# One operand of each routing step on VectorE in a bank of PSUM, in a kernel of attention, dense layers and routed experts

## The chip, the cores and the metric

The kernel runs on one core of one Trainium2 chip. The metric is the device time of one execution in microseconds (us). The engines are called PE (TensorE), DVE (VectorE), ACT (ScalarE), POOL (GpSimd) and SP (SyncE).

## What is computed

The reference chains three parts. First, attention over 4 batches and 8 heads with 1152 keys of 64 elements, where pairs of queries are averaged to 576. Then a dense block on the 2304 resulting tokens of 512 elements: `h = (x w1) * (x w2)`, `x2 = h w3 w_out`. Last, a mixture of 8 experts. The routing is greedy over all 2304 x 8 logits and is what the change touches:

```python
logits = x @ w_gate
order = np.argsort(-logits.flatten())
for idx in order:
    tok, e = (int(idx) // E, int(idx) % E)
    if assigned[tok] >= 0 or counts[e] >= cap:
        continue
    assigned[tok] = e
    counts[e] += 1
```

Each expert gets `cap` = 288 tokens and computes `relu(x w1[e]) w2[e]` for them.

## The kernel before, in words

**Who orders the work.** Nothing is issued in the order of the text. Every operation is handed to `Sched.op` (line 184) with its engine or engines, a cost in ns, a priority, and the keys that it reads and writes. `Sched.run` (line 214) then plays a model of the four engines with these costs and the latencies of `Sched.LAT`, always starts the ready operation of the lowest priority number, and emits the instructions of each engine in the order found. On the chip each engine's queue runs in that fixed order. Costs of `c_dve` (line 320) don't depend on what POOL does. The helper `call` of line 113 issues most instructions from attention onwards, so the trace shows L113 for them and groups are told apart by tile names.

**PSUM.** There are eight banks. Four, `pts` (tiles `pt0` to `pt3`, made at the start of `attention_moe_experts_kernel`), are handed out through `Slots` and `Hold`: an operation that `takes` a hold gets a free bank in the model, and the bank is free again after the hold's last user. The other four are `pb`, for matrix products. After attention the `pt` banks serve transposes (gathered rows into an expert, and an expert's result back into rows), the counts and small sums of the routing, the slot lists, and the products of the hidden units 4 up to `AHEAD` - 1 of expert 0 (line 1626). `AHEAD` is 7 (line 1723). With it, the products of units 0 to 6 with the left half of the gathered rows (`firsts`, line 1638) come before those with the right half.

**Stages from about 770 us on.** (1) The product W = w3 w_out on PE, split into two parts by ACT (`Wh`) and POOL (`Wl`). (2) x2 = h W, in 18 tiles of 128 tokens, with h split by ACT (`x2h`) and POOL (`x2l`). (3) The 8 experts: `unit` (line 1525) loads 128 rows of a weight into `u` and splits them into `uh` (ACT or DVE) and `ul` (DVE or POOL, u minus uh); `gather` (line 1584) fetches the expert's tokens by an indirect DMA on POOL's queue, transposes them on PE and splits them into `exh` and `exl`; `expert` (line 1621) multiplies on PE, splits the hidden units into `ehh` (ACT) and `ehl` (DVE), multiplies again, transposes back and scatters by an indirect DMA.

**Routing** (`routing`, line 853) runs beside all of these, with priority 1900 (W has 2000, x2 2010, the experts 3000). It has 8 phases. In a phase each token points to its best expert that is not full (`rt_m`, `rt_mu`, `rt_t`, `rt_mx`, `rt_oh`), and the logit value at which the first expert becomes full is found by a search in 8 rounds of 4 bits: 15 thresholds at a time are made (`rt_thr`, `rt_G`), all tokens are compared with them (`rt_mask`), PE counts by a matmul of `rt_oh` and `rt_mask`, DVE takes the right blocks out (`rt_cnt`, `rt_sum`, `rt_own` for the tile `rt_own8`), PE sums over partitions, and DVE finds how many thresholds hold (`rt_any`, `rt_flag`, `rt_n`) and extends the prefix (`rt_base`). After the rounds the phase assigns tokens and closes the expert (`rt_ge`, `rt_rows`, `rt_inc`, `rt_y`, `rt_r`, `rt_pen`, `rt_al`, `rt_acc`, `rt_s`, `rt_U`, `rt_rem`, `rt_pend`); `pick` chooses which closed expert is computed next and writes the row of its weights for SP's register; `lists` (in `slot_lists`, line 1069) turns the assignment into the indices `idx` of the gather. All of it is a chain of small fp32 or int32 instructions on DVE with two PE round trips per round, and all of its tiles lie in SBUF, but for what PE writes. The trace drops digits at the end of names: `rt_t` is t8 or t9, `rt_r` is r2, `rt_M` M or M1, `rt_acc` ac or ac2.

The tiles come from small rings; `make_ring` (line 130) hands out each name's buffers in turn, and the buffer is the key by which the planner orders readers and writers.

Of the kernel before, what the change touches and what calls it, by code (L numbers as in the profile page):

```python
# [11 lines left out]
F32 = mybir.dt.float32  # L12
# [839 lines left out]

def routing(nc, sch, rp, slots, c, L, keyL, A, rows_of, idx, prio, prio_l):

# [5 lines left out]
    def ring(name, n, shape, dt):  # L860
        return make_ring(sch, rp, "rt_" + name, n, shape, dt)

    r_m, r_mu = ring("m", 2, [128, NC], F32), ring("mu", 2, [128, NC], F32)
    r_t8, r_oh = ring("t8", 2, [128, NC, 8], F32), ring("oh", 2, [128, NC, 8], BF16)
    r_mx, r_mask = ring("mx", 1, [128, NC], F32), ring("mask", 2, [128, NC, NTHR], BF16)
    r_flag, r_any, r_n = ring("flag", 2, [128, NTHR], F32), ring("any", 2, [128, NTHR], F32), ring("n", 2, [128, 1], I32)
    r_cnt, r_sum = ring("cnt", 2, [NCG * NTHR, NCG, 8], F16), ring("sum", 2, [NCG * NTHR, 8], F16)
    own8 = rp.tile([97, NTHR, 8], F16, name="rt_own8")
    r_base, r_thr, r_G = ring("base", 2, [128, 1], I32), ring("thr", 2, [128, NTHR], I32), ring("G", 2, [128, NTHR], I32)
    r_M, r_M1 = ring("M", 1, [128, 1], I32), ring("M1", 1, [128, 1], I32)  # L870
    r_ge, r_rows = ring("ge", 1, [128, 2, 8, NC], F32), ring("rows", 1, [128, 16], BF16)
    r_inc, r_y = ring("inc", 1, [128, 8, NC], F32), ring("y", 1, [128, 8, NC], F32)
    r_r2, r_pen = ring("r2", 1, [128, 8], F32), ring("pen", 1, [128, 8], F32)
    r_al, r_acc, r_s = ring("al", 1, [128, 8], F32), ring("acc", 2, [128, 8, NC], F32), ring("s", 1, [128, NC], F32)
    U, keyU = ring("U", 1, [128, NC], F32)()
    rem, keyR = ring("rem", 1, [128, 8], F32)()
    pend, keyP = ring("pend", 1, [128, 8], F32)()
    r_sc, r_top, r_own = ring("sc", 1, [128, 8], F32), ring("top", 1, [128, 1], F32), ring("own", 2, [128, 8], F32)

    def dve(n, fn, r, w, engine="DVE", uses=(), pr=prio):  # L880
        sch.op(engine, c_dve(n) if engine == "DVE" else c_pool(n), fn, r=r, w=w, prio=pr, uses=uses)
# [4 lines left out]
    dve(120, lambda: nc.vector.memset(own8, 0.0), [], ["own8", "own8r"])  # L886
    dve(144, lambda: nc.vector.memset(A, 0.0), [], ["A"])
    dve(144, lambda: nc.vector.tensor_scalar(L, L, -1e34, 1e34, op0=OP.max, op1=OP.min), [keyL], [keyL])

    def pick(n):  # L890

        (sc, ksc), (top, kt), (own, ko) = r_sc(), r_top(), r_own()
        dve(8, lambda: nc.vector.scalar_tensor_tensor(sc, pend, 0.5, c["wd"], op0=OP.is_gt, op1=OP.mult), [keyP], [ksc], pr=P_PICK)
        dve(8, lambda: nc.vector.tensor_reduce(top, sc, axis=AX.X, op=OP.max), [ksc], [kt], pr=P_PICK)
        dve(8, lambda: nc.vector.tensor_scalar(own, sc, top, None, op0=OP.is_equal), [ksc, kt], [ko], pr=P_PICK)
        dve(8, lambda: nc.vector.tensor_tensor(pend, pend, own, op=OP.subtract), [keyP, ko], [keyP], pr=P_PICK)
        dve(4, lambda: nc.vector.scalar_tensor_tensor(
            rows_of[n], top[:, :].to_broadcast([128, 4]), -512.0, c["row"], op0=OP.mult, op1=OP.add), [kt], [("rows_of", n)], pr=P_PICK)
        return own, ko

    lists = slot_lists(nc, sch, rp, slots, c, A, idx, prio, prio_l)
    for ph in range(8):
# [6 lines left out]
        dve(18, lambda m=m, mu=mu: nc.vector.tensor_tensor(mu, m, U, op=OP.add), [km, keyU], [kmu])  # L909
        t8, kt8 = r_t8()  # L910
        dve(144, lambda m=m, t8=t8: nc.vector.tensor_tensor(
# [9 lines left out]
        if ph < 7:  # L921
# [4 lines left out]
            for rd, b in enumerate(BITS):  # L926
                T = 2 ** b - 1
                mask, kma = r_mask()
                if rd == 0:
                    thr, kth = c["t0"], "t0"  # L930
                else:
                    thr, kth = r_thr()
                    if rd == 1:
                        dve(T, lambda thr=thr, T=T, rd=rd, base=base: nc.vector.tensor_scalar(
                            thr[:, :T], c["grid"][rd][0], base, None, op0=OP.bitwise_xor), [kb], [kth])
                    else:
                        dve(T, lambda thr=thr, n=n, sh=sh, G=G: nc.vector.scalar_tensor_tensor(
                            thr, n[:, :].to_broadcast([128, NTHR]), sh, G, op0=OP.logical_shift_left, op1=OP.bitwise_xor), [kn, kG], [kth])
                    if rd + 1 < len(BITS):
                        G, kG = r_G()  # L940
                        dve(T, lambda G=G, rd=rd, base=base: nc.vector.tensor_scalar(
                            G, c["grid"][rd + 1][0], base, None, op0=OP.bitwise_xor), [kb], [kG])
# [63 lines left out]
            def f(ps=ps, rows=rows):  # L1006
# [3 lines left out]
            sch.op("PE", 40, f, r=[kro], takes=ps, prio=prio)  # L1010
            inc, kin = r_inc()
            dve(288, lambda ge=ge, inc=inc: nc.vector.tensor_tensor_scan(
# [17 lines left out]
                rem, pen, -1e-27, r2, op0=OP.mult, op1=OP.add), [kpe, kr2], [keyR])  # L1030
            ac, kac = r_acc()
            dve(144, lambda y=y, al=al, ac=ac: nc.vector.tensor_tensor(
# [12 lines left out]
        else:  # L1045
            un, kun = r_s()
            dve(18, lambda un=un: nc.vector.tensor_scalar(un, U, 0.0, None, op0=OP.is_equal), [keyU], [kun])
            t8, kt8 = r_t8()
            dve(144, lambda oh=oh, un=un, t8=t8: nc.vector.tensor_tensor(
# [18 lines left out]

def slot_lists(nc, sch, rp, slots, c, A, idx, prio, prio_l):

# [4 lines left out]

    r_all, r_s, r_rows = ring("all", 1, [128, NC, 8], F32), ring("s", 2, [128, NC], F32), ring("rows", 2, [128, 1], BF16)
    r_inc, r_pre, r_slot = ring("inc", 2, [128, NC], F32), ring("pre", 2, [128, 1], F32), ring("slot", 2, [128, NC], F32)
    r_ge, r_g, r_r = ring("ge", 2, [128, NC, 4], F32), ring("g", 2, [128, NC], F32), ring("r", 2, [128, NC], F32)
    r_oh, r_og = ring("oh", 1, [128, NC, 96], BF16), ring("og", 1, [128, NC, 3], F32)
# [59 lines left out]
def moe_and_experts(tc, sch, env, w1, w2, w3, w_out, w_gate, e1, e2, out):  # L1139
# [276 lines left out]
    rows_of = [rreg.tile([128, 4], I32, name=f"rows{n}") for n in range(8)]  # L1416
    routing(nc, sch, rreg, s_pt, rc, L, "L", A, rows_of, idx, P_R, P_L)

# [303 lines left out]
LIST_SLACK, RT_SLACK = 0.0, 0.0  # L1722
AHEAD = 7
HELD = 4
# [6 lines left out]
def attention_moe_experts_kernel(ctx, tc, q, k, v, w1, w2, w3, w_out, w_gate, e1, e2, out):  # L1731
# [10 lines left out]
    for r in regions.values():  # L1742
# [9 lines left out]
    env = {"nc": nc, "G": G, "xT": xT, "main": regions["main"], "prep": regions["prep"], "psS": regions["psS"],  # L1752
           "s_pt": s_pt, "ident": ident, "rc": rc, "xreg": regions["x"], "x2": dpool.tile([N, DM], F32, name="x2"), "x2a": dpool.tile([N, DM // 2], F32, name="x2a"), "w3t": dpool.tile([8, 128, 2, 1024], F32, name="w3t"),
           "wof": dpool.tile([8, 128, 2, DM], F32, name="wof")}
# [28 lines left out]
```

## Time and profile before

| | |
|---|---|
| median of 3 runs | 1267.52 us (1264.34 to 1271.21) |
| the profiled execution, its own time | 1259.13 us |
| its span, first to last instruction | 1257.3 us |
| mean granted clock of PE over the span | 0.977 |
| instructions | 24260 |
| the chain that ended last, by engine | PE 72%, DVE 21% |

The profile is of one execution. A page sums busy time by engine and groups instructions by line, engine, operation and tiles (`out<-in`). "Idle before" is the time that the engine waited just before such instructions, and the name behind an arrow is what ended most of it. Durations are those of one instruction from start to end; neighbours on an engine overlap by some tens of ns. [...] The chain that ended last is followed back from the last instruction: at each step to what released it, or to the instruction before it on its engine.

### The profile page before, as it was taken

What the parts mean: (1) busy time and instruction counts of PE and PEld (TensorE: products, weight loads), DVE (VectorE), ACT (ScalarE), POOL (GpSimd) and SP (SyncE); (2) the same over time, 40 slices, a digit from 0 to 9 for tenths busy, and PEclk for the clock granted to TensorE, in tenths of its full rate; (3) what the DMA queues carried; (4) which work ended last, traced back from release to release, by engine and by line L of the source; (5) the groups of instructions that cost most, each with busy time, mean ns of one, the idle gap of its engine ahead of it and who ended that gap; (6) DMA issues with size and microseconds to landing.
All of it is one profiled execution on the core that took longest, in us unless ns stands there. A gap on an engine that the chain in (4) does not pass through costs nothing.

```text
span 1257.3 us, 24260 instructions
## 1 busy us (share of the span) xinstructions
PE 1168.0 (93%) x8377; PEld 1099.2 (87%) x8377; DVE 1042.1 (83%) x2966; ACT 629.3 (50%) x1322; POOL 638.9 (51%) x649
## 2 busy tenths in 40 slices
PE   6999999999999999899999999988898868888997
PEld 4999999999999999899999998766677868888996
DVE  7999999999999999988777876778777988988741
ACT  6888888888888888333222202132221533322321
POOL 4566666666666765444332343264435654453730
PEclk9999999999999999899999999999997989998999
DMA  9676666666666541144555523432224644451620
GB/s 211 148 172 144 156 157 155 153 154 155 155 156 160 119 101 54 62 166 169 185 168 168 185 68 124 154 95 55 57 64 131 219 153 135 143 172 51 226 81 26
DMA packets 116618, 169.88 MB, mean 135 GB/s; under 512 B 47959, under 2 KB 79710, under 8 KB 116494
## 3 DMA queue, kind: packets, MB, share of 16 engines
q1 hardware_dynamic: 113326, 158.89, 46.9%
q0 software_dynamic: 3168, 9.44, 2.3%
q8 instruction: 66, 1.08, 0.4%
q14 instruction: 58, 0.48, 0.1%
HBM read 104.87 MB, written 24.45 MB: 103 GB/s over the span
## 4 chain that ended last, share of the span: by engine, by line
PE 72%; DVE 21%; issue 2%; DMA 2%; POOL 1%; ACT 1%; SPq 0%; DVEq 0%; POOLq 0%; ACTq 0%
PE pb L113 32%; PE s L590 12%; PE pt L614 7%; PE pt L664 6%; PE pt L113 5%; PE s L664 5%; PE s L614 3%; DVE ul L113 2%; DVE cv_v L113 2%; DVE rt_base L113 1%; DVE rt_flag L113 1%; DVE uh L113 1%; DVE rt_own L113 1%; DVE p L600 1%; DVE rt_mask L113 1%
## 5 line engine op out<-in xcount | busy, mean ns | idle before, releaser
L600 DVE TENSOR_SCALAR_CACHE_REDUCE p<-s 128x384 f32<-128x384 f32 x432 | 229.9, 551 | 32.6 <-PE pt L614 12.1
L590 PE MATMUL s<-kst,qst 128*128 128x384 f32 x768 | 198.7, 357 | 7.5 <-DVE p L600 4.0
L605 ACT ACTIVATE p<-p,mn 128x1152 f32<-128x1152 f32 x144 | 181.2, 1258 | 25.3 <-DVE mn L603 23.2
L113 PE MATMUL pb<-xhi,wh 128*128 128x288 f32 x512 | 156.6, 306 | 1.7 <-ACT wh L113 1.7
L113 PE MATMUL pb<-xlo,wh 128*128 128x288 f32 x512 | 152.5, 298 | 2.0 <-DVE xlo L113 2.0
L113 PE MATMUL pb<-xhi,wl 128*128 128x288 f32 x512 | 152.2, 297 | 1.1 <-DVE wl L113 1.1
L590 PEld LDWEIGHTS s<-kst,qst 128*128 128x128 f32 x768 | 122.5, 189 | 14.0 <-DVE p L600 10.6
L614 PE MATMUL pt<-ident,p 128*128 128x128 f32 x879 | 132.1, 272 | 0.3 <-ACT p L605 0.3
L113 POOL TENSOR_TENSOR ul<-u,uh 128x512 fp32r<-128x512 f32 (+1 forms) x45 | 88.9, 1984 | 77.7 <-ACT uh L113 30.2
L648 DVE TENSOR_TENSOR p_lo<-pt,p_hi 128x384 fp32r<-128x384 f32 x230 | 124.6, 551 | 0.7 <-ACT p_hi L331 0.7
L331 ACT ACTIVATE p_hi<-pt 128x384 fp32r<-128x384 f32 x230 | 106.6, 492 | 12.3 <-PE pt L614 12.1
L614 PEld LDWEIGHTS pt<-ident,p 128*128 128x128 f32 x879 | 106.8, 140 | 4.4 <-ACT p L605 0.5
L113 DVE SCALAR_TENSOR_TENSOR cv_v<-cv_raw,cv_v 128x512 int32<-128x512 int32 (+1 forms) x120 | 102.1, 856 | 6.7 <-POOL cv_raw L113 4.6
L113 PEld LDWEIGHTS pb<-xlo,wh 128*128 128x128 f32 x512 | 97.3, 190 | 2.8 <-DVE xlo L113 2.8
L113 PEld LDWEIGHTS pb<-xhi,wh 128*128 128x128 f32 x512 | 97.4, 190 | 2.6 <-ACT wh L113 1.9
L113 PEld LDWEIGHTS pb<-xhi,wl 128*128 128x128 f32 x512 | 97.3, 190 | 1.3 <-DVE wl L113 1.3
L341 POOL TENSOR_TENSOR p_lo<-praw,p_hi 128x384 fp32r<-128x384 f32 x96 | 96.9, 1017 | 0.4
L113 ACT ACTIVATE a<-pb 128x288 f32<-128x288 f32 x64 | 26.2, 410 | 132.4 <-PE pb L113 123.6
L335 POOL CAST p_hi<-praw 128x384 fp32r<-128x384 f32 x96 | 47.5, 506 | 83.3 <-ACT praw L331 83.2
L113 POOL TENSOR_TENSOR cv_raw<-cv_raw 128x512 f32<-128x512 f32 x40 | 43.2, 1079 | 86.5 <-DVE cv_v L113 67.3
L113 PE MATMUL pb<-exh,uh 128*128 128x288 f32 x244 | 78.6, 322 | 6.3 <-DVE ehl L113 6.3
L113 PE MATMUL pb<-ehh,uh 128*128 128x288 f32 x256 | 80.6, 315 | 0.0
(316 smaller groups left out, 3386.3 us busy)
## 6 DMA issues: line engine op xcount, KB each, us to landing
u<-in_moe_w_dram SPq DMA_DIRECT2D x64, 512.0 KB
cv_raw<-in_moe_w_dram SPq DMA_DIRECT2D x32, 512.0 KB
vr<-in_v_dram SPq DMA_DIRECT2D x32, 288.0 KB
kr<-in_k_dram SPq DMA_DIRECT2D x32, 288.0 KB
kst<-kH SPq DMA_DIRECT2D x31, 288.0 KB
kst<-kL SPq DMA_DIRECT2D x31, 288.0 KB
qr<-in_q_dram SPq DMA_DIRECT2D x15, 576.0 KB
w3t<-wg SPq DMA_DIRECT2D x16, 512.0 KB
```

The source lines that it names most:

```text
L113: return f(*[x.get() if isinstance(x, Lazy) else x for x in a], **{n: x.get() if isinstance(x, Lazy) else x for n, x in k.items()})
L331: nc.scalar.activation(out, in_, AF.Copy)
L335: nc.gpsimd.tensor_copy(out, in_)
L341: (nc.vector if eng == "DVE" else nc.gpsimd).tensor_tensor(out, a, b, op=OP.subtract)
L590: nc.tensor.matmul(ps.tile[:, :384], a[:, :], b[:, cs], start=(n == 0), stop=(n == len(passes) - 1))
L600: sch.op("DVE", c_dve(384), lambda ps=ps, c=c, cs=cs: nc.vector.tensor_scalar(t[:, cs], ps.tile[:, :384], 1.0, BIG, op0=OP.mult, op1=OP.mi ...
L605: sch.op("ACT", c_act(S, psum=False, acc=True), lambda: nc.scalar.activation(t, t, AF.Exp, bias=mn[:, 3:4], scale=-1.0, accum_out=sm[0][:, ...
L614: nc.tensor.transpose(ps.tile[:, a * 128:(a + 1) * 128], t[:, b * 128:(b + 1) * 128], ident)
L648: sch.op("DVE", c_dve(384), lambda view=view, src=src: nc.vector.tensor_tensor(view(lo), src(), view(hi).bitcast(F32), op=OP.subtract), us ...
L664: nc.tensor.matmul(ps.tile[:, :n], vt[:, t, :, :], src[half][:, t, off:off + n], start=(half == 0 and t == 0), stop=(half == 1 and t == NT ...
```

## The change

Most small tiles of the routing and the lists move from SBUF into one bank of PSUM, `pts[3]`: a new helper `in_bank` cuts them from the bank's 512 words per partition, words 0 to 143 being shared by the three large ones (`rt_t8p`, `rt_incp`, `rt_acp`), which live one after the other. They are chosen so that of two operands of a step one lies in the bank. Where a step reads two large tiles, its first result goes to the bank and its second stays in SBUF (t8 to the bank, t9 to SBUF; ac and ac2 alike). `rt_sum` becomes fp32 (it was fp16), several rings go from two buffers to one, and two constants, the grid of round 1 and the weights `wd`, are copied into the bank at the start. From the routing on, `Slots` is made of the first three banks alone, and `AHEAD` goes from 7 to 6. The computation is the same.

```diff
+def in_bank(bank, name, n, shape, dt, at=None):
+
+    size = int(np.prod(shape[1:]))
+    if at is None:
+        at = bank[1]
+        bank[1] += n * size
+        assert bank[1] <= 512
+    state = [0]
+
+    def nxt():
+        i = state[0] % n
+        state[0] += 1
+        t = bank[0][:shape[0], at + i * size:at + i * size + size]
+        t = t if dt == F32 else t.bitcast(dt)
+        t = t if len(shape) == 2 else t.rearrange("p (a b) -> p a b", a=shape[1])
+        return t, (name, i)
+    return nxt
...
-def routing(nc, sch, rp, slots, c, L, keyL, A, rows_of, idx, prio, prio_l):
+def routing(nc, sch, rp, slots, bank, c, L, keyL, A, rows_of, idx, prio, prio_l):
...
-    r_m, r_mu = ring("m", 2, [128, NC], F32), ring("mu", 2, [128, NC], F32)
-    r_t8, r_oh = ring("t8", 2, [128, NC, 8], F32), ring("oh", 2, [128, NC, 8], BF16)
-    r_mx, r_mask = ring("mx", 1, [128, NC], F32), ring("mask", 2, [128, NC, NTHR], BF16)
-    r_flag, r_any, r_n = ring("flag", 2, [128, NTHR], F32), ring("any", 2, [128, NTHR], F32), ring("n", 2, [128, 1], I32)
-    r_cnt, r_sum = ring("cnt", 2, [NCG * NTHR, NCG, 8], F16), ring("sum", 2, [NCG * NTHR, 8], F16)
+    at = lambda name, n, shape, dt: in_bank(bank, "rt_" + name, n, shape, dt)
+    r_m, r_mu = at("m", 1, [128, NC], F32), at("mu", 1, [128, NC], F32)
+    r_t8p, r_acp, r_incp = (in_bank(bank, "rt_big", 1, [128, NC * 8], F32, 0) for _ in range(3))
+    r_t8, r_oh = ring("t8", 1, [128, NC, 8], F32), ring("oh", 2, [128, NC, 8], BF16)
+    r_mx, r_mask = at("mx", 1, [128, NC], F32), ring("mask", 2, [128, NC, NTHR], BF16)
+    r_flag, r_any, r_n = at("flag", 1, [128, NTHR], F32), at("any", 1, [128, NTHR], F32), ring("n", 2, [128, 1], I32)
+    r_cnt, r_sum = ring("cnt", 2, [NCG * NTHR, NCG, 8], F16), at("sum", 1, [NCG * NTHR, 8], F32)
...
-    r_base, r_thr, r_G = ring("base", 2, [128, 1], I32), ring("thr", 2, [128, NTHR], I32), ring("G", 2, [128, NTHR], I32)
-    r_M, r_M1 = ring("M", 1, [128, 1], I32), ring("M1", 1, [128, 1], I32)
+    r_base, r_thr, r_G = at("base", 2, [128, 1], I32), ring("thr", 2, [128, NTHR], I32), at("G", 2, [128, NTHR], I32)
+    r_M, r_M1 = at("M", 1, [128, 1], I32), ring("M1", 1, [128, 1], I32)
+    (grid1, _), (wd, _) = at("grid1", 1, [128, NTHR], I32)(), at("wd", 1, [128, 8], F32)()
...
-    r_inc, r_y = ring("inc", 1, [128, 8, NC], F32), ring("y", 1, [128, 8, NC], F32)
-    r_r2, r_pen = ring("r2", 1, [128, 8], F32), ring("pen", 1, [128, 8], F32)
-    r_al, r_acc, r_s = ring("al", 1, [128, 8], F32), ring("acc", 2, [128, 8, NC], F32), ring("s", 1, [128, NC], F32)
+    r_y = ring("y", 1, [128, 8, NC], F32)
+    r_r2, r_pen = ring("r2", 1, [128, 8], F32), at("pen", 1, [128, 8], F32)
+    r_al, r_acc, r_s = at("al", 1, [128, 8], F32), ring("acc", 1, [128, 8, NC], F32), at("s", 1, [128, NC], F32)
...
-    r_sc, r_top, r_own = ring("sc", 1, [128, 8], F32), ring("top", 1, [128, 1], F32), ring("own", 2, [128, 8], F32)
+    r_sc, r_top, r_own = at("sc", 1, [128, 8], F32), at("top", 1, [128, 1], F32), at("own", 2, [128, 8], F32)
...
+    dve(NTHR, lambda: nc.vector.tensor_copy(grid1, c["grid"][1][0]), [], ["rt_consts"])
+    dve(8, lambda: nc.vector.tensor_copy(wd, c["wd"]), [], ["rt_consts"])
...
-        t8, kt8 = r_t8()
+        t8, kt8 = r_t8p()
+        t8 = t8.rearrange("p (c e) -> p c e", e=8)
...
-            inc, kin = r_inc()
+            inc, kin = r_incp()
+            inc = inc.rearrange("p (e c) -> p e c", e=8)
...
-            ac, kac = r_acc()
+            ac, kac = r_acp()
+            ac = ac.rearrange("p (e c) -> p e c", e=8)
...
-def slot_lists(nc, sch, rp, slots, c, A, idx, prio, prio_l):
+def slot_lists(nc, sch, rp, slots, bank, c, A, idx, prio, prio_l):
...
-    r_all, r_s, r_rows = ring("all", 1, [128, NC, 8], F32), ring("s", 2, [128, NC], F32), ring("rows", 2, [128, 1], BF16)
-    r_inc, r_pre, r_slot = ring("inc", 2, [128, NC], F32), ring("pre", 2, [128, 1], F32), ring("slot", 2, [128, NC], F32)
-    r_ge, r_g, r_r = ring("ge", 2, [128, NC, 4], F32), ring("g", 2, [128, NC], F32), ring("r", 2, [128, NC], F32)
+    at = lambda name, n, shape, dt: in_bank(bank, "sl_" + name, n, shape, dt)
+    r_all, r_s, r_rows = ring("all", 1, [128, NC, 8], F32), at("s", 1, [128, NC], F32), ring("rows", 2, [128, 1], BF16)
+    r_inc, r_pre, r_slot = ring("inc", 2, [128, NC], F32), ring("pre", 2, [128, 1], F32), at("slot", 2, [128, NC], F32)
+    r_ge, r_g, r_r = ring("ge", 2, [128, NC, 4], F32), ring("g", 2, [128, NC], F32), at("r", 1, [128, NC], F32)
...
-    routing(nc, sch, rreg, s_pt, rc, L, "L", A, rows_of, idx, P_R, P_L)
+    bank = [env["pts"][3], 144]
+    s_pt = Slots(env["pts"][:3])
+    routing(nc, sch, rreg, s_pt, bank, rc, L, "L", A, rows_of, idx, P_R, P_L)
...
-AHEAD = 7
+AHEAD = 6
```

## Rows read from the trace of the kernel before

**Rows 1.** The page, part 1: busy us and share of the span by engine.

```profile
PE 1168.0 (93%) x8377; PEld 1099.2 (87%) x8377; DVE 1042.1 (83%) x2966; ACT 629.3 (50%) x1322; POOL 638.9 (51%) x649
```

**Rows 2.** Windows: stretch, length, busy us by engine, granted clock, DMA share.

```profile
770.00:830.00 60.00, 54.13 (x273) 40.95 (x271) 44.94 (x160) 16.29 (x28) 22.82 (x21) 0.98 0.48 156
830.00:945.00 115.00, 103.76 (x568) 80.11 (x568) 86.66 (x307) 29.57 (x52) 52.23 (x44) 0.98 0.24 56
945.00:1150.00 205.00, 165.74 (x1235) 158.77 (x1234) 180.40 (x496) 65.17 (x125) 106.32 (x87) 0.91 0.45 146
1150.00:1257.00 107.00, 96.36 (x750) 94.80 (x749) 55.07 (x113) 27.75 (x54) 41.31 (x44) 0.96 0.34 113
```

**Rows 3.** PE's waits, 770 us on: us in total, times, longest.

```profile
PE pt L113 <- DVE rt_mask L113: 19.9, 18, 4.0
...
PE pb L113 <- DVE ehl L113: 6.5, 2, 6.3
```

**Rows 4.** Chain that ended last, 945 to 1150: start us, us, what.

```profile
970.48 2.10 DVE rt_base L113
...
1051.33 1.60 PE pb L113 x12
...
1142.93 2.46 DVE rt_ge L113 x2
```

**Rows 5.** Timeline from 1005 us, DVE then POOL: start, us, engine, what.

```profile
1008.03 2.83 DVE L113 TENSOR_SCALAR rt_pen<-rt_r 128x8 f32<-128x8 f32 x1
...
1012.25 2.32 DVE L113 SCALAR_TENSOR_TENSOR rt_U<-rt_s,rt_U 128x18 f32<-128x18 f32 x1
...
1008.41 2.42 POOL L113 TENSOR_TENSOR ul<-u,uh 128x1024 fp32r<-128x1024 f32 x1
...
1012.12 4.71 POOL L113 TENSOR_TENSOR ul<-u,uh 128x1024 fp32r<-128x1024 f32 x2
```

**Rows 6.** DVE groups by form from 770 us: xcount, busy us, mean ns, idle.

```profile
L113 DVE TENSOR_SCALAR rt_flag<-rt_any 128x15 f32<-128x15 f32 x56 | 27.2, 486 | 1.4
...
L113 DVE SCALAR_TENSOR_TENSOR rt_base<-rt_n,rt_base 128x1 int32<-128x1 int32 x49 | 20.3, 414 | 1.3
...
L113 DVE TENSOR_SCALAR rt_G<-rc_g,rt_base 128x15 int32<-128x15 int32 x42 | 17.9, 425 | 0.0
...
L113 DVE TENSOR_TENSOR rt_oh<-rt_t,rt_mx 128x144 bf16<-128x144 f32 x8 | 3.0, 376 | 0.0
```

**Rows 7.** Single tiles: ns min/median/max, first and last start, forms.

```profile
L113 DVE TENSOR_SCALAR rt_flag<-rt_any x56: 152/175/2083, 780.4 to 1137.6; 128x15 f32<-128x15 f32 x56
L113 DVE TENSOR_REDUCE rt_n<-rt_flag x56: 150/169/171, 780.6 to 1140.2; 128x1 int32<-128x15 f32 x56
...
L113 DVE SCALAR_TENSOR_TENSOR rt_base<-rt_n,rt_base x49: 147/160/2651, 785.4 to 1140.7; 128x1 int32<-128x1 int32 x49
L113 DVE TENSOR_SCALAR rt_G<-rc_g,rt_base x42: 217/234/3030, 781.6 to 1128.3; 128x15 int32<-128x15 int32 x42
```

**Rows 8.** Single tiles, and from the groups one write without a read.

```profile
L113 DVE SCALAR_TENSOR_TENSOR ehl<-pb,ehh x61: 435/448/459, 975.5 to 1234.3; 128x288 fp32r<-128x288 f32 x61
...
L113 DVE TENSOR_TENSOR rt_r<-pt,rt_rem x7: 152/158/160, 811.9 to 1146.9; 128x8 f32<-128x8 f32 x7
...
L113 DVE SCALAR_TENSOR_TENSOR rt_sc<-rt_pend,rc_wd x8: 152/154/161, 815.3 to 1151.5; 128x8 f32<-128x8 f32 x8
...
L113 DVE MEMSET rt_U<- 128x18 f32 x1 | 0.1, 73 | 0.0
```

**Rows 9.** POOL's `ul` by form, DVE's `ul` and `uh` as single tiles.

```profile
L113 POOL TENSOR_TENSOR ul<-u,uh 128x1024 fp32r<-128x1024 f32 x22 | 56.7, 2581 | 55.4 <-PE pb L113 22.0 <-ACT uh L113 16.9 <-PE pt L113 8.2
...
L113 DVE TENSOR_TENSOR ul<-u,uh x39: 676/1208/3260, 972.6 to 1208.0; 128x1024 fp32r<-128x1024 f32 x22, 128x512 fp32r<-128x512 f32 x17
...
L113 DVE CAST uh<-u x24: 409/680/2797, 968.8 to 1205.3; 128x1024 fp32r<-128x1024 f32 x14, 128x512 fp32r<-128x512 f32 x10
```

**Rows 10.** Windows, on `pt` alone: PE, weight loads, DVE, ACT busy.

```profile
945.00:1150.00 205.00, 37.25 (x318) 17.47 (x156) 26.37 (x91) 14.05 (x35) 0.91 0.45 146
```

More of the change, by code (lines that the diff above doesn't have):

```diff
@@ L892, in pick @@
         (sc, ksc), (top, kt), (own, ko) = r_sc(), r_top(), r_own()
-        dve(8, lambda: nc.vector.scalar_tensor_tensor(sc, pend, 0.5, c["wd"], op0=OP.is_gt, op1=OP.mult), [keyP], [ksc], pr=P_PICK)
+        dve(8, lambda: nc.vector.scalar_tensor_tensor(sc, pend, 0.5, wd, op0=OP.is_gt, op1=OP.mult), [keyP, "rt_consts"], [ksc], pr=P_PICK)
         dve(8, lambda: nc.vector.tensor_reduce(top, sc, axis=AX.X, op=OP.max), [ksc], [kt], pr=P_PICK)
@@ L899, in pick @@
         return own, ko
-    lists = slot_lists(nc, sch, rp, slots, c, A, idx, prio, prio_l)
+    lists = slot_lists(nc, sch, rp, slots, bank, c, A, idx, prio, prio_l)
     for ph in range(8):
@@ L934, in routing @@
                         dve(T, lambda thr=thr, T=T, rd=rd, base=base: nc.vector.tensor_scalar(
-                            thr[:, :T], c["grid"][rd][0], base, None, op0=OP.bitwise_xor), [kb], [kth])
+                            thr[:, :T], grid1, base, None, op0=OP.bitwise_xor), [kb, "rt_consts"], [kth])
                     else:
@@ L1047, in routing @@
             dve(18, lambda un=un: nc.vector.tensor_scalar(un, U, 0.0, None, op0=OP.is_equal), [keyU], [kun])
-            t8, kt8 = r_t8()
+            t8, kt8 = r_t8p()
+            t8 = t8.rearrange("p (c e) -> p c e", e=8)
             dve(144, lambda oh=oh, un=un, t8=t8: nc.vector.tensor_tensor(
@@ L1752, in attention_moe_experts_kernel @@
     env = {"nc": nc, "G": G, "xT": xT, "main": regions["main"], "prep": regions["prep"], "psS": regions["psS"],
-           "s_pt": s_pt, "ident": ident, "rc": rc, "xreg": regions["x"], "x2": dpool.tile([N, DM], F32, name="x2"), "x2a": dpool.tile([N, DM // 2], F32, name="x2a"), "w3t": dpool.tile([8, 128, 2, 1024], F32, name="w3t"),
+           "s_pt": s_pt, "pts": pts, "ident": ident, "rc": rc, "xreg": regions["x"], "x2": dpool.tile([N, DM], F32, name="x2"), "x2a": dpool.tile([N, DM // 2], F32, name="x2a"), "w3t": dpool.tile([8, 128, 2, 1024], F32, name="w3t"),
            "wof": dpool.tile([8, 128, 2, DM], F32, name="wof")}
```

## The prediction, on record before the run

> **What bounds the kernel now.** I read the page's busy shares first [rows 1]: PE 93%, VectorE (DVE) 83%, POOL 51%. Such shares mix stages, so I cut the span at the stages the names give: routing beside the weight product (770 to 830 us), routing beside x2 (830 to 945), routing beside the experts (945 to 1150), experts alone (1150 to the end) [rows 2]. Before 770 us the change has no instruction. Each row gives the stage's length, then each engine's busy time. The last stage is PE's: 96.4 of 107 us. The third is not: PE is busy for 165.7 of 205 us, DVE for 180.4, and PE's granted clock is 0.91 on average. Only there do PE's 39 us of idle time and DVE's work stand against each other.
>
> Next, whom PE waited for from 770 us on [rows 3]: matmuls of the counts wait 19.9 us in all for `rt_mask`, and in two pieces 6.5 us for `ehl`; nearly all other waits also end at a DVE result. PE's queue is in order, so a count matmul whose mask is late holds the expert matmuls behind it. The chain that ended last says why the mask is late [rows 4]: between 945 and 1150 us it holds 19 pieces of over 1 us on routing tiles of DVE (the first and the last stand there), 37.8 us in sum. These instructions work on 1 to 270 elements per partition. The timeline shows one such place [rows 5]: `rt_pen`, 8 elements, takes 2.83 us and ends at 1010.86, when POOL's `ul` (1008.41 + 2.42) ends at 1010.83; `rt_U` takes 2.32 us beside the next two `ul`. Of all DVE instructions after 770 us, 79 last over 0.1 us longer than is usual in their group; each overlaps a POOL TENSOR_TENSOR with two operands in SBUF.
>
> How much is it? By form [rows 6] against the medians [rows 7]: `rt_flag` 56 x (486 - 175 ns) = 17.4 us, `rt_base` 49 x (414 - 160) = 12.4; 18 more groups of routing and lists, worked the same way from `rt_G` (42 x (425 - 234) = 8.0) down to `rt_oh` (0.6), add 44. That is 74 us of standing still. Who never stands still: `rt_n`, a reduction with one operand, 150 to 171 ns in all 56 cases [rows 7], though it stands between `rt_flag` and `rt_base`; and whatever reads one operand from PSUM, as `ehl` (435 to 459 ns in 61 cases) and `rt_r` (152 to 160) [rows 8]. These run in the same stages beside the same POOL work.
>
> **The change, part by part.**
>
> Operands moved. In each phase some 55 results are written to the bank and about 105 instructions read or write it, 759 in seven phases and the short eighth (counted in the code: 71 in the eight rounds, 19 around them, 5 in `pick`, 10 in a list). No DVE instruction of the rounds then works on SBUF alone. By the rows of `ehl` and `rt_r` one that reads PSUM doesn't wait for POOL. One that reads its one tensor from SBUF and writes PSUM (`rt_G` and `rt_pen` will, 8.0 and 2.6 us of the stall) has no row; I let it go too, as it is nearer to `rt_n` than to a pair of operands, and keep 10.6 x 33/72 = 5 us of span for the range's upper end. What stays as it is are `rt_inc` (1.2 us of the stall) and `idx` (0.6). So about 72 us of stall go from DVE. On the chain it is less: of the 37.8 us, 19 undisturbed pieces at about 0.25 us would remain, so **33 us** go from the third stage.
>
> Who is late next. POOL's pieces last as long as before, and DVE's own `ul` and `uh` splits still have their operands in SBUF: 39 and 24 instructions [rows 9] in some 313 us, one each 5 us. POOL runs 22 `ul` of 2.58 us [rows 9], and about as many of half that. One of 2.58 us catches a split in half the cases and holds it for half its length: 22 x 0.5 x 1.3 = 14 us, and a third of it, some 5, for the short ones. The groups of `ul` and `uh`, worked as above, lose 11.6 us already (longest 3260 ns against a median of 1208 [rows 9]). So I give back **8 us**, an estimate from these rows.
>
> First two stages. PE is idle there for 5.9 and 11.2 us [rows 2], and DVE for 43: each waits for the other, and PE has x2's matmuls in front of most counts. Half of the waits for the mask are round trips of about 0.5 us that no stall made. I take a third of PE's 17 us: **6 us**.
>
> Clock. [...] I take **4 us** back.
>
> One bank fewer. Three banks serve transposes, counts and lists. In the third stage all work on them is busy for 37.3 us on PE, 26.4 on DVE and 14.1 on ACT [rows 10], 78 us in 205, or 0.4 bank on average; waiting may double that. The cover is gone only where expert 0 holds banks: two of three in place of three of four, one free as before. `AHEAD` 6 takes one early half group of expert 0 out of the wait for the gather: 6 matmuls, at 12 in 1.60 us [rows 4] 0.8 us. With two copies at the start (15 and 8 elements, 0.15 us each by `rt_sc` [rows 8]) and a little for plans that shift: **+1.5 us**. A count that finds no bank would hold the round, and the expert matmuls behind it.
>
> Price of the bank. Reads: `rt_r` reads PSUM, `rt_sc` the same 8 elements from SBUF, 158 against 154 ns [rows 8]; I take zero. Writes by DVE to PSUM stand nowhere in the trace. The bound is an instruction that only writes: MEMSET of 18 elements 73 ns [rows 8], some 55 without the elements. About 400 of the 759 write the bank: between -22 and +22 us of DVE time, and at the share of the stall that lies on the chain (33 of 72) between -10 and +10 of the span. I take zero, as the reads show no difference, and keep both ends.
>
> [...]
>
> Sum: 33 - 8 + 6 + 4 - 1.5 = 33.5 us less. The profiled execution took 1259.1 us (span 1257.3 and 1.8 around it), which gives 1225.6. The median of the runs, 1267.5, is 8.4 above it, so I forecast **1234** in those terms; the times below are in them too. About 0.5% (6.3 us) is what a measurement of this kernel can tell from no change.
>
> **Rivals.**
>
> The stall moves. If nearly every POOL `ul` piece catches a split instead, 63 x 1.3 us / 2 = 41 us of stall in place of 11.6: give-back about 29, all else small, leaves 33 - 29 + 10 = 14 less: 1253. For it: 63 splits stand in DVE's queue [rows 9]. Against: they came into only 9 such waits before.
>
> More than the stall. Once DVE has slack, PE runs nearly gap-free at full clock in the third stage: 39 us idle, less about 9 for the gather and round trips, with 12 from the first two stages and 10 of clock, 52 less: 1216. For it: stage four shows PE at 96.4 of 107. Against: eight rounds of DVE to PE to DVE a phase remain.
>
> The bank costs on reads too. At 55 ns (the MEMSET) on each of 759 instructions, 42 of the 72 us come back; 33.5 x 30/72 = 14 less: 1254. Against: [rows 8]. [...]
>
> Slower: the same price, but of a whole small instruction. If writing and reading back through the bank makes each dependent step wait 155 ns longer (`rt_sc` once more), 759 x 155 = 118 us against 72, and 46 x 33/72 = 21 more: 1289. It decides from 72/759 = 95 ns on. For it: the write is unseen. Against: PSUM readers' rows, and 95 ns is more than the MEMSET's whole 73.
>
> No change: a mixed pair of operands waits for POOL all the same, and the 61 quiet `ehl` are luck: 1267.
>
> **How the numbers follow.** Forecast 0.54, more than the stall 0.13, stall moves 0.16, reads cost 0.06, slower 0.06, no change 0.05. Faster by over 0.5% (below 1261) are the first four: 0.89; same 0.05; slower 0.06. The range runs from 1213 (the second case with a little less clock loss) to 1258 (the two small gains, and the forecast with 10 for the writes and 5 for `rt_G`, 1249); it leaves out about 0.14.
>
> **What would show it.** Right: `rt_flag`, `rt_base` and `rt_G` within 20 ns of their medians with maxima under 0.3 us; routing pieces over 1 us gone from the chain; the third stage near 175 us with DVE busy near 150; clock above 0.93. The price of the bank: `rt_flag` and `rt_base` at 175 and 160 ns, or above. Give-back: `ul` and `uh` means above 1361 ns and their maxima more frequent. Banks: PE's waits before `pt` that end at an `eo`, `exh` or `exl` reader. I am wrong if these instructions still reach 2 us, or if they are short and the third stage stays near 205.

## The result, and the profile after

| | before | after |
|---|---|---|
| median of the runs side by side | 1269.37 us (1264.34 to 1276.66) | 1231.76 us (1230.55 to 1232.78) |
| ratio, 95% interval | | 0.9699 (0.9648 to 0.975) |
| the profiled execution, its span | 1259.13, 1257.3 us | 1232.52, 1230.7 us |
| mean granted clock | 0.977 | 0.988 |

The change is faster by 3.0%; 1234 us was forecast. The sum of busy times on the page (part 1), against [rows 1]: DVE has 38 us less to do, PE the same work at a better clock.

```profile
PE 1160.5 (94%) x8377; PEld 1090.8 (89%) x8377; DVE 1003.9 (82%) x2968; ACT 630.8 (51%) x1322; POOL 628.9 (51%) x649
```

The windows of [rows 2] in the changed kernel (the last ends with its shorter span):

```profile
770.00:830.00 60.00, 56.91 (x293) 43.09 (x292) 42.97 (x170) 17.50 (x31) 22.86 (x21) 1.00 0.50 161
830.00:945.00 115.00, 106.13 (x630) 83.90 (x629) 84.75 (x345) 30.16 (x55) 53.63 (x52) 1.00 0.30 70
945.00:1150.00 205.00, 181.19 (x1385) 173.24 (x1385) 171.96 (x510) 73.33 (x139) 114.75 (x100) 0.95 0.49 161
1150.00:1230.00 80.00, 69.69 (x525) 68.62 (x524) 31.32 (x54) 18.48 (x36) 21.27 (x24) 0.95 0.28 91
```

In the same 205 us PE does 15.5 us more than before and 150 more matmuls, at a clock of 0.95 in place of 0.91. DVE was the busier engine there; now PE is.

The groups of DVE by form, from 770 us. A tile in the bank is shown as `pt`, so `rt_flag` is the third line, `rt_base` the fifth, `rt_G` the second. Columns: count, busy us and mean ns, idle before.

```profile
L113 DVE TENSOR_REDUCE pt<-pt 128x15 f32<-128x120 f32 x56 | 16.2, 288 | 26.8 <-PE pt L113 26.2
L113 DVE TENSOR_SCALAR pt<-rc_g,pt 128x15 int32<-128x15 int32 x42 | 10.1, 240 | 1.3
L113 DVE TENSOR_SCALAR pt<-pt 128x15 f32<-128x15 f32 x56 | 10.1, 180 | 1.5
L113 DVE TENSOR_REDUCE rt_n<-pt 128x1 int32<-128x15 f32 x56 | 9.6, 172 | 1.5
L113 DVE SCALAR_TENSOR_TENSOR pt<-rt_n,pt 128x1 int32<-128x1 int32 x49 | 8.0, 163 | 1.4
L113 DVE TENSOR_TENSOR_SCAN pt<-rc_rst,rt_ge 128x144 f32<-128x144 f32 x7 | 6.0, 864 | 0.0
```

Against [rows 6]: `rt_flag` went from a mean of 486 ns to 180, `rt_base` from 414 to 163, `rt_G` from 425 to 240. Their longest are 182, 165 and 243 ns, where [rows 7] had over 2 us. Worked as in the prediction (each instruction against the usual length of its group), routing and lists lose 4.1 us in place of 74. Of that the scan `rt_inc`, which still reads two tiles of SBUF, has 2.9 and `idx` 1.2: the two that the prediction had named as staying. All 20 DVE instructions after 770 us that still last over 0.1 us too long overlap a two-operand subtraction or product of POOL, as all but two of those before did.

What was to be late next is the splits of the experts' weights, here as single tiles (min/median/max), to be held against [rows 9]:

```profile
L113 DVE TENSOR_TENSOR ul<-u,uh x39: 672/1216/2784, 957.4 to 1180.2; 128x1024 fp32r<-128x1024 f32 x22, 128x512 fp32r<-128x512 f32 x17
```

And pieces of the chain that ended last, 945 to 1150 us (start, us, what):

```profile
971.74 5.52 DMA u<-in_moe_w_dram
...
999.93 1.65 DVE pt L113
...
1058.52 1.41 DVE pt L113
...
1077.42 2.70 DVE ul L113
...
1110.55 2.45 DVE uh L113
...
1139.81 7.73 DMA u<-in_moe_w_dram
```

Of the 19 pieces of over 1 us on routing tiles in [rows 4] three are left: `rt_inc` twice (the lines with `pt`) and `idx` with 1.05 us. `ul` and `uh` have taken their place. Their groups lose 16.6 us, 11.6 before. New on the chain are four loads of weights (`DMA u`), 21.6 us in all, of which two are shown; before, the chain had none. No experiment is about them; in the fastest kernel of run 6 they are 4.3 us. Whom PE waits for changes with that (us in all, times, longest), against [rows 3]:

```profile
PE pt L113 <- DVE exl L113: 10.0, 7, 2.7
PE pt L113 <- DVE rt_oh L113: 6.0, 6, 1.5
...
PE pt L113 <- DVE rt_mask L113: 3.5, 7, 0.7
```

The wait for the mask fell from 19.9 us to 3.5.

### The profile page after: what moved, and what is told of

It reads as the page before. It is cut to its first block, busy times and chain, and to the rows that moved or that the text cites. A ratio compares the mean times of both kernels' runs of the same rounds, so it can differ in the third digit from the quotient of the medians.

```text
span 1230.7 us, 24265 instructions
## 1 busy us (share of the span) xinstructions
PE 1160.5 (94%) x8377; PEld 1090.8 (89%) x8377; DVE 1003.9 (82%) x2968; ACT 630.8 (51%) x1322; POOL 628.9 (51%) x649
## 4 chain that ended last, share of the span: by engine, by line
PE 73%; DVE 20%; DMA 3%; issue 2%; POOL 1%; ACT 1%; SPq 0%; DVEq 0%; POOLq 0%; ACTq 0%
PE pb L113 32%; PE s L590 12%; PE pt L614 7%; PE pt L664 6%; PE pt L113 6%; PE s L664 5%; DVE pt L113 4%; PE s L614 3%; DMA u<-in_moe_w_dram 2%; DVE cv_v L113 2%; DVE ul L113 1%; DVE uh L113 1%; DVE p L600 1%; DVE sl_oh L113 1%; DVE ehl L113 1%
## 5 line engine op out<-in xcount | busy, mean ns | idle before, releaser
L600 DVE TENSOR_SCALAR_CACHE_REDUCE p<-s 128x384 f32<-128x384 f32 x432 | 230.0, 551 | 34.9 <-PE pt L614 11.6
L331 ACT ACTIVATE p_hi<-pt 128x384 fp32r<-128x384 f32 x230 | 106.8, 493 | 11.8 <-PE pt L614 11.6
```

What stands on the lines that cost most here:

```text
L331: nc.scalar.activation(out, in_, AF.Copy)
L600: sch.op("DVE", c_dve(384), lambda ps=ps, c=c, cs=cs: nc.vector.tensor_scalar(t[:, cs], ps.tile[:, :384], 1.0, BIG, op0=OP.mult, op1=OP.mi ...
```

## The experiments

The theory: PSUM operands keep DVE from standing still beside POOL, and that is the gain. Rivals: the gain comes from the other plan that three banks bring, or the bank has a price that hides in it. Every ratio is to the kernel before in runs on the same chip.

**1. Every small tile back in SBUF.** The order of the instructions on every engine is that of the changed kernel; only the places differ.

```diff
-    r_m, r_mu = at("m", 1, [128, NC], F32), at("mu", 1, [128, NC], F32)
+    r_m, r_mu = ring("m", 1, [128, NC], F32), ring("mu", 1, [128, NC], F32)
...
-    r_base, r_thr, r_G = at("base", 2, [128, 1], I32), ring("thr", 2, [128, NTHR], I32), at("G", 2, [128, NTHR], I32)
+    r_base, r_thr, r_G = ring("base", 2, [128, 1], I32), ring("thr", 2, [128, NTHR], I32), ring("G", 2, [128, NTHR], I32)
```

> The changed kernel with every small tile of the routing back in SBUF: the order of the instructions on all engines, the three banks and AHEAD 6 stay those of the changed kernel, so only the place of the operands differs. Theory (the gain is the waiting beside POOL's TENSOR_TENSORs): the stall of the routing on DVE returns to 60 to 80 us and the time to 1260 to 1278 us. Rival (the gain is in the new order and the banks): 1245 us or less. If both have a share, between them.

Measured: 1272.25 us (1269.14 to 1277.12), ratio 1.0033 (1.0009 to 1.0058). The groups by form:

```profile
L113 DVE TENSOR_SCALAR rt_flag<-rt_any 128x15 f32<-128x15 f32 x56 | 27.9, 498 | 1.5
L113 DVE SCALAR_TENSOR_TENSOR rt_base<-rt_n,rt_base 128x1 int32<-128x1 int32 x49 | 15.1, 308 | 1.4
L113 DVE TENSOR_SCALAR rt_G<-rc_g,rt_base 128x15 int32<-128x15 int32 x42 | 13.4, 319 | 0.0
```

The stall of routing is back, 74.6 us in all, and so is the time. The placement alone gives 40.5 us (1272.25 to 1231.76), and the plan that comes with it gives nothing: with it and SBUF tiles the kernel takes some 4 us more than the kernel before (ratio 1.0033).

**2. One bank fewer, and nothing else:** the kernel before with three banks and `AHEAD` 6.

```diff
+    s_pt = Slots(env["pts"][:3])
...
-AHEAD = 7
+AHEAD = 6
```

> The kernel before with three banks for transposes, counts and lists and AHEAD 6, and nothing else of the change. If the bank that is taken away costs little, as the prediction had it (+1.5 us), 1266 to 1271 us; with the other plan and its price as the whole change with its tiles in SBUF showed, 1271 to 1275; a gain (below 1264) would say that the fourth bank was no use.

Measured: 1265.08 us (1261.69 to 1269.06), ratio 0.9977 (0.9959 to 0.9994). That is just under the first range. The fourth bank cost nothing when it went; if anything the kernel is a little faster without it. The 4 us that run 1 took more than the kernel before are thus not the banks as such.

**3. Only the tiles of the rounds in the bank:** `rt_mu`, `rt_sum`, `rt_any`, `rt_flag`, `rt_base`, `rt_G`, `rt_M` and the grid; all others are back in SBUF (the edit is as in 1).

> The changed kernel with only the tiles of the eight rounds in the bank (mu, sum, any, flag, base, G, M, the grid), the other steps of a phase, the pick and the lists in SBUF; the order on all engines is that of the changed kernel. The rounds' groups held about 51 of the 74 us of stall before. Theory, with the gain in proportion: 1240 to 1250 us, stall of the routing about 20 us. Rival (the steps between the rounds lie alone on the chain and count for more): 1250 to 1260 us. Rival (the rounds alone are the chain): 1231 to 1236 us.

Measured: 1242.87 us (1238.9 to 1244.32), ratio 0.9803 (0.9768 to 0.9838). The stall of routing is 24.9 us: a part of the tiles brings a part of the gain, in the range that the theory gave.

**4. No reads by POOL.** POOL's subtractions for W, x2 and the experts' weights become three MEMSETs of about the same length in all (the one MEMSET of 1408 elements on POOL took 1.27 us in the kernel before, so three with 2560 in all about 2.3, an estimate, against 2.58 for an `ul` of 1024); the kernels leave out the low parts that POOL would have made. This is done to the kernel before, to the changed one, and to that of run 1. A MEMSET has nothing to read (the trace names no operand, as for `rt_U<-` in [rows 8]), so a second thing goes as well: in the changed kernel POOL waits for the high parts before it subtracts (in the line below `ul` for ACT's `uh`: us, times, longest; `x2l` for `x2h` 38.8 us), and with MEMSETs it doesn't. No run parts the two.

```profile
POOL ul L113 <- ACT uh L113: 46.3, 16, 9.1
```

```diff
-        sch.op(None, {e: costl[e] for e in lo_e}, lambda eng: sub(eng, lo(), src(), hi().bitcast(F32)),
-               r=list(r) + [wh], w=[wl], prio=pr, uses=us)
+        stage = sch.label
+
+        def low(eng):
+            if eng != "POOL" or stage not in ("W", "x2", "exp"):
+                return sub(eng, lo(), src(), hi().bitcast(F32))
+            a = lo().bitcast(F32)
+            for part in (a, a, a[:, :a.shape[1] // 2]):
+                nc.gpsimd.memset(part, 0.0)
+        sch.op(None, {e: costl[e] for e in lo_e}, low, r=list(r) + [wh], w=[wl], prio=pr, uses=us)
```

> The kernel before, in its own order, with POOL's subtractions for the low parts of W, h and the experts' weights replaced by memsets of zero of about the same length (2.4 us for 1024 elements, in three pieces); the low parts that POOL makes are left out. All operands of the routing stay in SBUF. Theory: DVE waited because POOL read SBUF; rt_base, rt_own, rt_U and rt_mu (two operands in SBUF) keep to their medians, and the time falls to 1220 to 1240 us. rt_flag and rt_G, with one operand, tell whether they wait for POOL's writes too: if they do, some 25 us of stall stay and the time is 1240 to 1255. Rival (any work of POOL in SBUF holds DVE, or the gain is in the order): 1260 to 1275 us.

Measured: 1199.11 us (1198.09 to 1201.24), ratio 0.947 (0.9441 to 0.95), lower than expected, though `rt_flag` still waits beside MEMSETs (294 ns in the mean, 175 its median before; the routing still loses some 17 us). Standing still beside POOL's reads, that of the splits with it, and POOL's own waits are together worth 69 us; how much of that is the standing still isn't shown.

> The changed kernel with POOL's subtractions replaced by memsets as in the kernel before: what is left of the waiting. DVE's ul and uh lose 16.6 us in the changed kernel, the routing 4. Theory: ul keeps to its medians (two operands in SBUF), and the time falls by 5 to 12 us to 1220 to 1227. Rival (this waiting is beside the chain): 1229 to 1233 us. Rival (uh, one operand, waits for POOL's writes as for its reads): uh's mean stays near 1000 ns, and half of the gain is missing.

Measured: 1213.35 us (1212.82 to 1213.54), ratio 0.9575 (0.9548 to 0.9603), lower than expected too, and yet 14 us slower than the same edit on SBUF tiles.

> The changed kernel's three banks for transposes, its AHEAD 6 and its order of instructions, but with every small tile of the routing in SBUF, and POOL's subtractions for W, x2 and the experts' weights replaced by three MEMSETs each, so nobody stands still beside them. It leaves out the low parts that POOL would have made. With the bank the same thing took 1213.4 us, and the kernel before's order with four banks 1199.1. If the 14 us between them are the three banks and the other plan, this run takes 1210 to 1215 us; if they are the price of working on PSUM (5 to 20 ns on each of some 560 instructions in DVE's chain of rounds, which the durations bring to about 6 us), 1199 to 1207. I expect 1206, some of each.

Measured: 1195.77 us (1194.99 to 1199.03), ratio 0.944 (0.9413 to 0.9468). My guess of 1206 was wrong, and neither the banks nor the plan cost anything. This kernel and the one in the bank issue the same 2968 DVE instructions in the same order, so **17.6 us** (1213.35 to 1195.77; 17 by the ratios, as the two ran on different chips) are the price of the bank, and a net one. In SBUF the routing still loses about 16 us beside the MEMSETs, as in this group of the kernel in SBUF, and in the bank nothing:

```profile
L113 DVE TENSOR_SCALAR rt_flag<-rt_any 128x15 f32<-128x15 f32 x56 | 16.7, 298 | 1.5
```

So as far as these 16 us reach the end, the bank itself costs more than 17.6. The lengths of the instructions don't show this price: the medians of the routing differ by at most some 20 ns, for instance `rt_flag` 182 against 175. The timeline of DVE does (start us, length us), first in the bank:

```profile
1009.96 0.17 DVE L113 TENSOR_REDUCE rt_n<-pt 128x1 int32<-128x15 f32 x1
1010.17 0.16 DVE L113 SCALAR_TENSOR_TENSOR pt<-rt_n,pt 128x1 int32<-128x1 int32 x1
1010.37 0.17 DVE L113 SCALAR_TENSOR_TENSOR rt_thr<-rt_n,pt 128x15 int32<-128x15 int32 x1
1010.57 0.24 DVE L113 TENSOR_SCALAR pt<-rc_g,pt 128x15 int32<-128x15 int32 x1
1010.85 0.44 DVE L113 TENSOR_TENSOR rt_mask<-pt,rt_thr 128x270 bf16<-128x270 f32 x1
```

The last four of these steps in SBUF:

```profile
1007.08 0.15 DVE L113 SCALAR_TENSOR_TENSOR rt_base<-rt_n,rt_base 128x1 int32<-128x1 int32 x1
1007.15 0.16 DVE L113 SCALAR_TENSOR_TENSOR rt_thr<-rt_n,rt_G 128x15 int32<-128x15 int32 x1
1007.26 0.23 DVE L113 TENSOR_SCALAR rt_G<-rc_g,rt_base 128x15 int32<-128x15 int32 x1
1007.41 0.43 DVE L113 TENSOR_TENSOR rt_mask<-rt_mu,rt_thr 128x270 bf16<-128x270 f32 x1
```

From the start of `rt_base` to that of the mask it is 0.68 us in the bank and 0.33 in SBUF. `rt_thr` takes nothing from `rt_base`, and in SBUF it starts some 80 ns before `rt_base` ends. In the bank it starts 34 ns after that end, 116 ns more on average of the 42 cases, and the trace records there a wait for DVE's own semaphore, which the instruction in SBUF doesn't have. The bank is one tile to the program, and each access waits for the last one there, when one of the two writes, whatever words they use. In the trace, of the 507 neighbours from 770 us on that both touch the bank and of which one writes it, none overlap (34 ns apart in the median, 472 with such a wait). Of the 88 that only read it, 82 overlap, by 83 ns in the median and without a wait for DVE's semaphore. So it is the wait that keeps them apart, and not the work on PSUM as such. From 770 us on there are 264 places where an instruction overlaps the one before it in SBUF and follows 20 to 50 ns behind its end in the bank; they sum to 34 us of DVE's time. The net 17.6 us at the end are half of that.

**5. The splits off DVE.** The high parts on ACT alone, and then the low parts on POOL alone as well:

```diff
-        lo_e, hi_e = (("POOL",), ("ACT",)) if first else (("DVE", "POOL"), ("ACT", "DVE"))
+        lo_e, hi_e = (("POOL",) if first else ("DVE", "POOL")), ("ACT",)
```

> The changed kernel with the high parts of the experts' weights made by ACT alone (the low parts by DVE or POOL as before). The 24 CASTs of DVE that POOL's subtractions hold are gone. My theory: DVE loses about 8 us of standing still and 15 us of work, ACT has the room, and the time is 1223 to 1229 us. The rival: ACT, in order, makes the high parts later behind its other work, PE waits for weights in the stage of experts, and it takes 1232 to 1245 us.

Measured: 1223.05 us (1218.53 to 1226.97), ratio 0.9652 (0.9626 to 0.9678), as the theory had it.

> The changed kernel with the experts' weights split by ACT (high part) and POOL (low part) alone, so that nothing of DVE that POOL's subtraction can hold is left but rt_inc and idx. My theory: some 17 us of standing still and some 60 us of work leave DVE, PE becomes the bound of the third stage, and the time is 1218 to 1226 us. The rival: POOL, with 63 subtractions of 1.3 to 2.6 us in place of about 40, is the late one, the weights come late, and it takes 1240 us or more.

Measured: 1222.31 us (1220.41 to 1224.76), ratio 0.9638 (0.9611 to 0.9665). In the range, but not better than the run before it. POOL is busy for 58 us more, and the stall finds SBUF instructions that are left, above all `idx` (min/median/max):

```profile
L113 DVE SCALAR_TENSOR_TENSOR idx<-sl_fl x8: 149/210/5473, 824.4 to 1108.2; 96x3 int32<-96x3 f32 x8
```

Eight instructions of three elements lose 13.3 us. What is taken out of POOL's way in one place is caught in the next.

**6. The order of the search.** `rt_base` and `rt_G` of rounds 1 to 6 after the next mask, in place of before it (the old lines that go are left out here):

```diff
                 dve(NC * T, lambda mask=mask, thr=thr, T=T, mu=mu: nc.vector.tensor_tensor(
                     mask[:, :, :T], mu[:, :, None].to_broadcast([128, NC, T]),
                     thr[:, None, :T].bitcast(F32).to_broadcast([128, NC, T]), op=OP.is_ge), [kmu, kth], [kma])
+                if later:
+                    nb, knb = r_base()
+                    dve(1, lambda n=n, nb=nb, sh=sh, base=base: nc.vector.scalar_tensor_tensor(
+                        nb, n, sh, base, op0=OP.logical_shift_left, op1=OP.bitwise_xor), [kn, kb, kma], [knb])
+                    base, kb, later = nb, knb, False
+                if 0 < rd < len(BITS) - 1:
+                    G, kG = r_G()
+                    dve(T, lambda G=G, rd=rd, base=base: nc.vector.tensor_scalar(
+                        G, c["grid"][rd + 1][0], base, None, op0=OP.bitwise_xor), [kb, kma], [kG])
```

> The order with base and G after the mask, in the bank, with POOL's subtractions for W, x2 and the experts' weights replaced by three MEMSETs each, so nobody stands still; it leaves out those low parts. The bank without this order took 1213.4 us, SBUF with the same plan 1195.8. If most of the 17.6 us between them is base and G in front of the mask, 1196 to 1203 us; if it is longer instructions all along, 1208 to 1213.

Measured: 1206.03 us (1204.34 to 1208.73), ratio 0.9509 (0.9484 to 0.9534), between the two ranges. Taking these two out from in front of the mask gives back 7.3 of the 17.6 us.

> The changed kernel, with rt_base and rt_G of rounds 1 to 6 worked out after the mask of the next round in place of before it; rt_thr and the mask don't need them. My theory of the bank's hidden price: an instruction that touches the bank starts only 34 ns after the one before it that wrote there, wanted or not, where on SBUF it started 80 ns before that one's end; so base (198 ns from start to start) and G (275) hold the mask by 473 ns in 42 rounds, 20 us of DVE's chain, and about 0.7 of it lies on the path, as the other pair of kernels suggests: 1215 to 1223 us. The rival: the rounds are hidden beside the experts' matmuls (PE waits for the mask only 3.6 us in all), and it stays at 1229 to 1233 us.

Measured: 1231.78 us (1228.95 to 1233.29), ratio 0.9705 (0.9684 to 0.9726): the rival's number, no gain. But not for its reason that the rounds are hidden in any case, as the run above and the last one show. The splits lose more here (columns as above):

```profile
L113 DVE TENSOR_TENSOR ul<-u,uh 128x1024 fp32r<-128x1024 f32 x24 | 37.8, 1580 | 0.7 <-ACT uh L113 0.4
L113 DVE TENSOR_TENSOR ul<-u,uh 128x512 fp32r<-128x512 f32 x15 | 18.6, 1242 | 1.7 <-ACT uh L113 1.5
```

They lose 23.2 us in all in place of 16.6, and `idx` 2.6 in place of 1.2. The plan shifts the splits into POOL's subtractions, 8 us more of standing still; that this ate the gain is argued, not shown.

> The kernel before (SBUF, four banks) with base and G after the mask. There they take about 77 and 145 ns from start to start, and the stall of the two (12.4 and 8.0 us) leaves the way to the mask, though not DVE. By my theory half of the 20 us of stall and 7 of the 9 us of work leave the path: 1245 to 1256 us. If the stall only moves to the instructions that then stand beside POOL, 1260 to 1268 us. Were it as fast as the bank with this order (1215 to 1223), the bank itself would be of no use.

Measured: 1264.28 us (1262.99 to 1270.26), ratio 0.9968 (0.9946 to 0.999). My theory was wrong, and the rival's range holds: the stall of routing stays at 74.1 us. It finds other instructions: `rt_base` loses 3.3 us in place of 12.4, and `rt_own` 13.7 in place of 6.6. The order alone is no substitute for the bank.

> The order of the run before (base and G after the mask), and the high parts of the experts' weights on ACT alone. If the two gains add up (9 us from ACT's high parts, some 12 from the order), 1208 to 1215 us; if PE is the bound by then, 1216 to 1223 us.

Measured: 1216.17 us (1213.82 to 1218.15), ratio 0.9582 (0.9562 to 0.9602). This is the fastest kernel that computes everything, 15.6 us below the changed kernel and 52 below the one before. It lies in the range given for PE as the bound, and the two gains don't add up. With the high parts off DVE, the order is worth 7 us (1223.05 to 1216.17). Window of the third stage:

```profile
945.00:1150.00 205.00, 190.31 (x1470) 183.92 (x1470) 170.41 (x506) 92.34 (x164) 107.33 (x98) 0.95 0.54 178
```

PE is busy for 9 us more there than in the changed kernel, and ACT for 19 more: it had the room.

## Why the prediction was right, and where it was not

The runs of 1 and 4 take the change apart. From run 1 (all in SBUF, 1272.25) the bank leads to 1231.76; MEMSETs for POOL's subtractions to 1213.35; and the tiles back in SBUF to 1195.77. These steps are 40.5, 18.4 and 17.6 us. The first is the place of the operands alone. The second is what the splits still lose together with POOL's waits for the high parts. The third is the price of the bank, net of what SBUF tiles still lose beside MEMSETs.

- **Operands moved: right.** 72 of 74 us of stall were to go; 70 went. That each of the 79 late instructions stood beside a TENSOR_TENSOR of POOL holds for all but two: `rt_flag` at 951.03 us and `uh` at 1053.24 had only its indirect DMAs or a MEMSET beside them, and lost under 0.2 us each. `rt_G` and `rt_pen`, one operand in SBUF and the result in the bank, don't wait (means of 240 and 169 ns, the longest 243 and 170): the 5 us kept for them were not needed.
- **The stall on the path: too small.** I took 33 of 72 us, with 6 and 4 for the first stages and the clock: 43. PE's busy time in the first two windows grew by 5.2 us (2.8 and 2.4). So the 6 about holds. No run shows the 4 for the clock, nor the 10 in the rival "more than the stall"; the traces show the time at a granted clock of 0.5 in the third stage go from 35.4 us to 20.7 (the mean there from 0.91 to 0.95), and PE busy for 6 us less in all four windows together (420.0 to 413.9). The chain's share was too little: with a price of the bank of 17.6, the 40.5 us that came by the medians would be 58 without it. Why is argued, not shown: a chain names one path, and a stall of DVE that is not on it can still make the masks of later rounds late.
- **Price of the bank: wrong,** and this is the step that failed: "I take zero, as the reads show no difference". It is 17.6 us of span, net, beyond the bound of 10. I priced lengths, and lengths hardly changed. The price is between the instructions, where neighbours that overlapped now follow each other. The rival "slower" had the place right, a longer step from one dependent instruction to the next, but put 155 ns on all 759; it is about 130 (34 us over 264) on about a third of them. `rt_base` and `rt_thr`, 150 to 170 ns long, overlap by some 80 ns in SBUF, where no wait stands between them; with the wait the second starts 34 ns after the first has ended.
- **One bank fewer: too high.** +1.5 us was said; run 2 is 2.9 us below its kernel before (0.9959 to 0.9994).
- **Who is late next: right in kind, small in measure.** Splits lose 16.6 us in place of 11.6, so 5 and not 8 more, far from the 29 of the rival. But their whole stall, the old part included, may be worth up to 18.4 us, the difference that MEMSETs make to the changed kernel; POOL's waits are part of that.
- **The third stage** was to be near 175 us with DVE busy for 150, a share of 0.86; the share is 0.84 (171.96 of 205).

So it was luck that the forecast of 1234 came out 2 us off: by the medians two terms missed by some 15 us each and in opposite directions, too little for the stall and too little for the bank. Luck was in the base too. The forecast took 33.5 us from the profiled execution (1259.1 to 1225.6) and then added the 8.4 us by which the median lay above it. The profiled execution after took 1232.52 us, only 26.6 us less, but its median lies no higher (1231.76).

## What to carry to other kernels

Where one engine stands still beside another's work in SBUF, as DVE does beside POOL's here, look at the small instructions on the critical chain: one operand in PSUM took these out of the stall (74 us to 4.1). Then look which instructions of the other kind are left, because part of the stall goes to them (`ul` and `uh` lost 16.6 us here, 11.6 before). Price small instructions by the distance from start to start and not by length: where a bank is one tile to the program, as here, small tiles in it are ordered against each other even where no data passes (`rt_thr` 34 ns after the end of `rt_base`, in SBUF 80 before it). So take what the next step doesn't need out from between its inputs and it; with MEMSETs for POOL's subtractions, that gave back 7.3 of 17.6 us here.

## What the runs showed of the hardware

DVE's instructions with one operand from SBUF (TENSOR_SCALAR, CAST) stand still here even beside POOL's MEMSETs. In the kernel before with MEMSETs, from 770 us on, 35 of 144 TENSOR_SCALARs and 12 of 25 CASTs last over 0.1 us too long, but only 6 of the 439 TENSOR_TENSORs and SCALAR_TENSOR_TENSORs that work on SBUF alone; with POOL's subtractions it was 43 of the 439. The groups by form of that run:

```profile
L113 DVE TENSOR_SCALAR rt_flag<-rt_any 128x15 f32<-128x15 f32 x56 | 16.5, 294 | 1.4
L113 DVE TENSOR_REDUCE rt_n<-rt_flag 128x1 int32<-128x15 f32 x56 | 9.3, 166 | 1.4
L113 DVE SCALAR_TENSOR_TENSOR rt_base<-rt_n,rt_base 128x1 int32<-128x1 int32 x49 | 7.7, 157 | 1.3
L113 DVE TENSOR_SCALAR rt_pen<-rt_r 128x8 f32<-128x8 f32 x7 | 3.0, 433 | 0.0
```

`rt_base`, the worst but one before with a mean of 414 ns, is clean at 157; `rt_flag` and `rt_pen` are not, at 294 and 433 (medians before 175 and 172). Of the 230 reductions 1 is too long. In the bank none of them waits: with MEMSETs the 7 instructions of the changed kernel that are still too long are all CASTs of the splits.
